# First matmuls on zeros counted at half clock in the plan, identity made on the chip, constants issued first, and the small matmuls on them later

## The chip, the cores and the metric

The kernel runs on one core of a Trainium2 chip. The time is the device time of one execution in microseconds (us). Eight runs of the kernel before gave a median of 177.66 us, the lowest 175.87 and the highest 178.57: six of them lie between 177.46 and 178.57, two at 175.87 and 176.14. One further execution was profiled; it took 177.76 us, of which the recorded span is 176.0 us.

A core has five engines that run side by side and wait for each other by semaphores: PE (TensorE; its weight loads are the row PEld), DVE (VectorE), ACT (ScalarE), POOL (GpSimd) and SP (SyncE, which here only issues transfers). Each engine takes its instructions in the order in which the program gives them, so an instruction that waits also holds up all that stands behind it.

## The reference

A retention layer is followed by a channel mix. Shapes: q, k, v are 4 batches x 8 heads x 768 steps x 64; the mix has a model width of 512 and an inner width of 1024.

```python
for t in range(S):
    state = gamma[None, :, None, None] * state + np.einsum('bhd,bhe->bhde', k[:, :, t], v[:, :, t])
    y[:, :, t] = scale * np.einsum('bhd,bhde->bhe', q[:, :, t], state)
...
x_prev = np.concatenate([np.zeros((B, 1, D), dtype=np.float32), x[:, :-1, :]], axis=1)
xk = mu_k * x + (1.0 - mu_k) * x_prev
xr = mu_r * x + (1.0 - mu_r) * x_prev
k = np.maximum(xk @ w_k, 0.0)
v = k * k @ w_v
r = 1.0 / (1.0 + np.exp(-(xr @ w_r)))
return (r * v).astype(np.float32)
```

## The kernel before

**Tiling.** Each batch is cut into six chunks of 128 steps, and the recurrence is done for two chunks at once, so there are 12 windows, here called w0 to w11. For a window, 512 KB each of k, q and v are loaded (L402). k and q are cast to half precision (L425 on DVE or L426 on ACT, `qks`), transposed on PE against an identity (L433), and copied out of PSUM (L443, `qkT`); v is multiplied by its decay (L456, on POOL or DVE). PE then forms the state (L475, L486; scaled by DVE at L499), the attention of each pair of steps (L519; masked by DVE at L536 with `causal2`), and the output (L561 from the state, L579 from the masked attention). DVE multiplies the output by `Gy` into `xT` (L599). One L579 is a Y below, with the window's number: Y0, Y1, Y2.

For the channel mix DVE forms the difference of neighbouring steps (`dx`, L623) and with `mu` the two mixed inputs `xk` and `xr` (L631). PE multiplies `xk` by `wk` (L662, "Z"), ACT takes the relu (L676, `krel`) and the square (L683, tile `k`); PE multiplies `xr` by `wr` (L695, "R"), ACT takes the sigmoid (L708, `rsb`); PE multiplies the squares by `wv` (L702, "V"), DVE multiplies both (L713, `osb`) and SP stores the result (L717).

**Weights.** `wk` comes in two halves, `wr` whole, `wv` in two halves: five transfers of 1024 KB (L376) into float32 tiles `w`, of which there are two (`w32=2`), so the third transfer needs the first tile cast, the fourth the second, and so on. A cast to half precision (L378 on DVE, L379 on ACT, L380 on POOL) fills a fifth of the weights that stay. The first V (L702) needs both halves of `wv`.

**Constants.** c32 (16 KB: the decays and a small identity `eye8`), c16 (96 KB: the 128x128 identity and the causal mask), c2 (9 KB) and two rows of mu (2 KB each) are issued by ACT's queue (L327). Two float32 matmuls on c2 (L358) and two copies (L361) make `Gy`; one transpose on `eye8` (L364) and a copy (L366) make `mu`.

**The plan.** No order is written out by hand. Tasks with a due time (`key`), buffers and ways (an engine, a duration, an added cost) are put to `Plan.order()`, which plays the program through with durations from the source and fixes, for each engine, the order of its instructions. `BUFS` says how many buffers of each kind there are, `COST` shifts the choice between engines, `FIRST` gives the due times of the first transfers, `LAT` the time that one engine's result takes to another, `STORE` by how much a store is put off, and `BLOCKS` how many chunks one channel-mix step takes in a batch. What is planned decides the order only; on the chip semaphores decide the time.

**Matmuls on zeros.** Where PE would stand idle in the first 60 us of the plan's time, `order()` puts in matmuls on a tile of zeros (`warm`, L280, a 128x256 one each), which nothing reads. They are there to hold the clock of PE. They are fixed in PE's order like the rest.

The lines that matter below:

```python
21  LA = (2, 0.3, 4)
66      FILL = 110
108             r = max(r, a.end + self.LAT[a.eng])
168                             f.start, f.end, f.eng = now, now + self.FILL, "PE"
269     ident = c16[:, 0:P]
435             e_T = add(key + 0.02 * i, pe(450, do_T), after=[e_c, k_c16] + hist[-1:], takes=[pT, xT],
```

## Time and profile before

| from the profile of the execution of 177.76 us | |
|---|---|
| span | 176.0 us, so 1.76 us lie outside it |
| PE busy | 167.1 us (95%), 2341 matmuls, of which 120 on zeros (17.5 us) |
| PE, 50 to 172 us | busy for 122.00 of 122.00 us, none of it on zeros |
| DVE busy | 131.5 us (75%) |
| ACT busy | 105.2 us (60%) |
| POOL busy | 37.6 us (21%) |
| bytes moved | 30.87 MB; 264 to 384 GB/s in the slices from 4.4 to 48.4 us, 129 GB/s on average from 50 to 172 us |
| first V (L702) | starts at 39.85 us |
| last matmul ends | 172.2 us |

The span is the time from the first recorded instruction to the last. A share of busy time is an average over all of it. The kernel has two parts that must be read apart: a head, in which PE fills its gaps with matmuls on zeros and waits, and a body, in which it does neither. In a row of a timeline the first number is the start in us, the second the duration of the group, then engine, line, operation, output, input and how many; in brackets stands how long the engine was idle before it and what ended that.

### The profile page before, as it was taken

The page shows a single profiled execution, that of the slowest core. Times are in us where ns is not written, and L with a number is a line of the kernel's source. Part 1 is how long each engine was busy: PE and PEld are TensorE (multiplying, and loading weights), DVE is VectorE, ACT ScalarE, POOL GpSimd, SP SyncE. Part 2 cuts the span into 40 slices and gives each one's busy share as a digit, 9 for nine tenths or more (in the row PEclk, how much of TensorE's full clock was granted, in tenths as well). Part 3 has the DMA queues.
Part 4 walks back from the last instruction along what each step waited for, and adds up shares of the span by engine and source line. Part 5 has one row for each costly group of instructions (what it writes and reads, how often), then busy time and mean ns, then how long its engine had stood idle before and what let it go on. Part 6 is the DMA issues. An engine that isn't in the chain of part 4 may idle for free.

```text
span 176.0 us, 5321 instructions
## 1 busy us (share of the span) xinstructions
PE 167.1 (95%) x2341; PEld 112.3 (64%) x2341; DVE 131.5 (75%) x230; ACT 105.2 (60%) x140; POOL 37.6 (21%) x32
## 2 busy tenths in 40 slices
PE   7959998989999999999999999999999999999991
PEld 5546877755855856856757747658567666775850
DVE  0024699988889999989888888798888499895311
ACT  2634254793692883983955936947829753646560
POOL 0035050492200344422003024240040040000000
PEclk9978999999999999999999999999999999999998
DMA  5999999999949656673393574846411011110202
GB/s 142 311 384 302 345 295 305 319 292 287 264 141 248 181 155 200 192 228 108 139 239 106 161 218 133 247 125 217 123 60 63 0 63 60 63 60 22 101 26 93
DMA packets 43866, 30.87 MB, mean 175 GB/s; under 512 B 1210, under 2 KB 38210, under 8 KB 43844
## 3 DMA queue, kind: packets, MB, share of 16 engines
q1 hardware_dynamic: 43536, 30.41, 58.7%
q8 instruction: 18, 0.29, 0.7%
q10 hardware_dynamic: 308, 0.13, 0.3%
q14 instruction: 4, 0.03, 0.1%
HBM read 24.25 MB, written 6.29 MB: 174 GB/s over the span
## 4 chain that ended last, share of the span: by engine, by line
PE 89%; POOL 4%; DVE 4%; issue 2%; DVEq 0%
PE pm L662 24%; PE pm L702 24%; PE pm L695 12%; PE pm L280 7%; PE px L433 6%; PE px L579 4%; PE px L486 4%; PE px L519 4%; PE px L561 3%; POOL wv L380 3%; DVE v L456 2%; POOL v L456 1%; PE pm L358 1%; DVE dx L623 1%; PE px L475 1%
## 5 line engine op out<-in xcount | busy, mean ns | idle before, releaser
L662 PE MATMUL pm<-xk,wk 128*128 128x256 f16 (+1 forms) x480 | 47.7, 251 | 0.0
L702 PE MATMUL pm<-wv,k 128*128 128x512 f16 x192 | 45.4, 379 | 0.6 <-POOL wv L380 0.6
L662 PEld LDWEIGHTS <-wk 128*128 128x128 f16 x480 | 38.2, 98 | 6.4
L443 ACT COPY qkT<-px 128x1024 f16<-128x1024 f16 x24 | 24.1, 1010 | 30.0 <-PE px L433 30.0
L676 ACT ACTIVATE krel<-pm 128x512 f32<-128x512 f32 x48 | 28.3, 596 | 19.0 <-PE pm L662 18.6
L456 POOL TENSOR_TENSOR v<-t,c_sb 128x512 f16<-128x512 f32 x20 | 20.5, 1046 | 77.5 <-issue 55.6
L536 DVE TENSOR_TENSOR a2t<-px,c_sb 128x512 f16<-128x512 f32 x48 | 30.7, 683 | 1.3 <-PE px L519 1.0
L702 PEld LDWEIGHTS <-k 128*128 128x128 f16 x192 | 17.8, 98 | 20.2 <-issue 0.7
L713 DVE SCALAR_TENSOR_TENSOR osb<-pm,rsb 128x512 f32<-128x512 f32 x24 | 16.6, 691 | 16.1 <-PE pm L702 8.5
L631 DVE SCALAR_TENSOR_TENSOR xr<-dx,mu,xT 128x256 f16<-128x256 f32 x48 | 22.6, 520 | 3.4 <-PE pm L695 3.3
L695 PE MATMUL pm<-wr,xr 128*128 128x512 f16 x96 | 24.8, 380 | 0.0
L426 ACT CAST qks<-t 128x1024 f16<-128x1024 f32 x19 | 19.7, 1041 | 6.0 <-DMA t<-in_k_dram 4.6
L683 ACT ACTIVATE k<-krel 128x1024 f16<-128x1024 f32 x21 | 22.2, 1059 | 0.5
L631 DVE SCALAR_TENSOR_TENSOR xk<-dx,mu,xT 128x256 f16<-128x256 f32 x48 | 21.4, 496 | 0.4
L280 PE MATMUL pm<-warm 128*128 128x256 f16 x120 | 17.5, 298 | 1.1 <-DVE xT L588 1.1
L708 ACT ACTIVATE rsb<-pm 128x512 f32<-128x512 f32 x24 | 14.2, 594 | 5.7 <-PE pm L695 5.5
L599 DVE TENSOR_TENSOR xT<-px,Gy 128x512 f32<-128x512 f32 x24 | 15.4, 683 | 1.9 <-PE px L579 1.6
L433 PEld LDWEIGHTS <-qks 128*128 128x128 f16 x192 | 13.2, 102 | 4.0
L623 DVE TENSOR_TENSOR dx<-xT 128x1024 f32<-128x1024 f32 x12 | 15.3, 1272 | 0.1
L433 PE MATMUL px<-c_sb,qks 128*128 128x128 f16 x192 | 15.3, 227 | 0.0
L280 PEld LDWEIGHTS <-warm 128*128 128x128 f16 x120 | 12.0, 106 | 3.9 <-DVE xT L588 1.1
L499 DVE TENSOR_TENSOR s<-px,c_sb 128x512 f16<-128x512 f32 (+1 forms) x12 | 7.2, 602 | 7.8 <-PE px L486 7.6
(30 smaller groups left out, 102.9 us busy)
## 6 DMA issues: line engine op xcount, KB each, us to landing
t<-in_k_dram SPq DMA_DIRECT2D x12, 512.0 KB, 5.3
t<-in_q_dram SPq DMA_DIRECT2D x12, 512.0 KB, 4.7
t<-in_v_dram SPq DMA_DIRECT2D x12, 512.0 KB, 4.6
out_dram<-osb SPq DMA_DIRECT2D x24, 256.0 KB, 2.5
w<-in_moe_w_k_dram SPq DMA_DIRECT2D x2, 1024.0 KB, 8.8
w<-in_moe_w_v_dram SPq DMA_DIRECT2D x2, 1024.0 KB, 8.7
w<-in_moe_w_r_dram SPq DMA_DIRECT2D x1, 1024.0 KB, 9.7
c_sb<-c ACTq DMA_DIRECT2D x1, 96.0 KB, 5.0
```

The source lines that it names most:

```text
L280: nc.tensor.matmul(b.tile[:, 0:256], lhsT=warm[:, 0:P], rhs=warm, start=True, stop=True)
L426: act(1010, lambda a=cast_args: nc.scalar.copy(**a()), cost=COST["qk"])],
L433: nc.tensor.transpose(o[:, j, m], x16.tile[:, j, m], ident)
L443: act(1010, lambda o=xT_out, pT=pT: nc.scalar.copy(out=o(), in_=pT.tile.bitcast(F16))),
L456: return lambda: engine.tensor_tensor(out=v16.tile[:, hs], in0=t32.tile[:, hs], in1=Gv[:, hs].unsqueeze(3).broadcast_to([P, 4, 2, D]), op= ...
L536: dve(690, lambda i=a_in, o=a_out: nc.vector.tensor_tensor(out=o(), in0=i(), in1=causal2, op=ALU.mult)),
L631: (200 + TM) / 0.96, lambda w=w, o=o, co=co: nc.vector.scalar_tensor_tensor(out=cut(o)[:, co], in0=cut(dx)[:, co], scalar=mu[:, w * NCO + ...
L662: nc.tensor.matmul(o[:, n], lhsT=wk16[:, co, fo * P : fo * P + P], rhs=cut(xk)[:, co, t0 : t0 + TM], start=(co == 0), stop=(co == NCO - 1))
L676: act(600, lambda pZ=pZ, o=r_out: nc.scalar.activation(out=o(), in_=pZ.tile, func=AF.Relu, scale=KSC)),
L683: act(1060, lambda krel=krel, k2=k2: nc.scalar.activation(out=k2.tile, in_=krel.tile, func=AF.Square)),
L695: nc.tensor.matmul(pR.tile, lhsT=cut(xr)[:, co, t0 + ts.start : t0 + ts.stop], rhs=wr16[:, co, :], start=(co == 0), stop=(co == NCO - 1))
L702: nc.tensor.matmul(pV.tile, lhsT=o[:, n, ts], rhs=wv16[:, fo, :], start=(fo == 0), stop=(fo == NFO - 1))
```

## The change

Durations, lines of code and tasks are changed together:

- A matmul on zeros that the plan puts in before 1500 + 3600 ns of its time counts as 220 ns there, later ones as 110 ns.
- The identity is made on the chip by POOL, by a memset and an `affine_select`, and no longer loaded; c16 holds the mask alone (64 KB). The transposes no longer wait for c16; the masking does.
- c32, c2, c16 and mu are issued in this order at the head of ACT's queue; in the plan their results count as 4500 ns late instead of 2000.
- The matmuls that make `Gy` and `mu` get later due times, and in w0 they come after the first attention matmuls (L519).
- `FIRST`, `BUFS`, `COST`, `STORE` and `BLOCKS` have other values. Among these: 3 tiles for loads of q, k, v (`t32`) instead of 5, 2 of `krel` instead of 4, 4 of `k2` instead of 6, 5 of `rsb` instead of 7, 3 of `osb` instead of 2, 3 of `qks` instead of 2. In batch 0 the channel mix of the first four chunks is done chunk by chunk, with Z as 128x128 matmuls.

The planned order changes with these. In PE's order 122 matmuls on zeros stand instead of 120, and the first V comes after the same other work as before, but with 64 Z of 128x128 in place of 32 of 128x256. The weights are cast by ACT (both halves of `wk`, `wr`, one half of `wv`) and POOL (the other half of `wv`); before, POOL cast all five. ACT casts 22 of the tiles of q and k instead of 19 and takes 41 relus instead of 48, DVE 7 instead of none; DVE copies 4 of the 24 `qkT`. SP's transfers stand in this order: k0 q0 v0 wk k1 q1 v1 wk k2 q2 wr v2 wv wv k3; before it was k0 q0 v0 wk wk k1 q1 v1 wr k2 q2 v2 wv wv k3 (the number is the window's).

```diff
@@ -19,14 +19,14 @@
 
 
 LA = (2, 0.3, 4)
-BLOCKS = {0: ((2,), (2,), (2,)), 3: ((1, 1), (1, 1), (1, 1))}
+BLOCKS = {0: ((1, 1), (1, 1), (2,)), 3: ((1, 1), (1, 1), (1, 1))}
 BLOCKS_ELSE = ((2,), (2,), (2,))
-STORE = 4
-FIRST = "k0 mu q0 c2 c16 v2 c32 v0 v1 q1 q2 wk1 wk0 k1 wr k2 wv1 wv0".split()
+STORE = 3
+FIRST = "c32 c2 c16 v1 q0 q2 q1 mu k0 v0 wk1 k1 wk0 k2 wr v2 wv1 wv0".split()
 BY_ACT = ("c2", "c16", "c32", "mu")
-BUFS = dict(t32=5, qks=2, v16=1, qkT=4, a2t=5, s16=2, xT=2, dx=3, xk=2, xr=1, krel=4, k2=6,
-            rsb=7, osb=2, w32=2)
-COST = dict(qk=-500, qkT=1200, relu=1200, mask=2000, dx=2000, v=200, w=-200, wd=500, sq=-500)
+BUFS = dict(t32=3, qks=3, v16=1, qkT=4, a2t=5, s16=4, xT=3, dx=2, xk=3, xr=2, krel=2, k2=4,
+            rsb=5, osb=3, w32=2)
+COST = dict(qk=0, qkT=300, relu=200, mask=800, dx=500, v=300, w=0, wd=800, sq=-200)
 
 
 class Buf:
@@ -48,7 +48,7 @@
         self.key, self.ways, self.mode, self.follows = key, ways, mode, follows
         self.after = [a for a in after if a is not None]
         self.takes, self.uses = list(takes), list(uses)
-        self.start = self.end = self.eng = self.emit = None
+        self.start = self.end = self.eng = self.emit = self.lat = None
 
 
 class Way:
@@ -63,7 +63,7 @@
     LAT = {"PE": 240, "ACT": 80, "DVE": 80, "POOL": 120, "DMA": 2000, "SP": 0}
     SWITCH = 100
     REACH = 1.2
-    FILL = 110
+    FILL, COLD = 110, 3600
 
     def __init__(self, filler, fill, fill_tag):
         self.tasks, self.bufs, self.makers = [], {}, {}
@@ -105,7 +105,7 @@
             for a in t.after:
                 if a.end is None:
                     return None
-                r = max(r, a.end + self.LAT[a.eng])
+                r = max(r, a.end + (a.lat or self.LAT[a.eng]))
             if any(not b.taken for b in t.uses):
                 return None
             for n, b in enumerate(t.takes):
@@ -165,7 +165,8 @@
                             f = Task(0, [], (), [b], (), "full", None)
                             r = ready(f)
                             if r is not None and r <= now:
-                                f.start, f.end, f.eng = now, now + self.FILL, "PE"
+                                slow = 2 if now < self.fill[0] + self.COLD else 1
+                                f.start, f.end, f.eng = now, now + self.FILL * slow, "PE"
                                 f.emit = lambda b=b: self.filler(b)
                                 b.users = 1
                                 finish(f, e)
@@ -252,7 +253,7 @@
         axis=1).astype(np.float32)
     causal_np = np.concatenate(
         [tq[None, :] >= (2 * (np.arange(P) % 64) + i)[:, None] for i in range(2)], axis=1)
-    c16_np = np.concatenate([np.eye(P), causal_np], axis=1).astype(np.float16)
+    c16_np = causal_np.astype(np.float16)
 
     const_pool = ctx.enter_context(tc.tile_pool(name="consts", bufs=1))
     c32d = nc.inline_tensor(c32_np, name="c32")
@@ -266,8 +267,8 @@
     c2 = const_pool.tile([2, c2_np.shape[1]], F32, name="c2_sb")
     Gy = const_pool.tile([P, 2, NJ, C], F32, name="Gy")
     eye8 = c32[0:8, o + 2 * NJ : o + 2 * NJ + 8]
-    ident = c16[:, 0:P]
-    causal2 = c16[:, P : P + 2 * C].unsqueeze(1).broadcast_to([P, 2, 2 * C])
+    ident = const_pool.tile([P, P], F16, name="ident")
+    causal2 = c16.unsqueeze(1).broadcast_to([P, 2, 2 * C])
     murow = const_pool.tile([8, P], F32, name="murow")
     mu = const_pool.tile([P, 8], F32, name="mu")
     wk16 = const_pool.tile([P, NCO, dff], F16, name="wk16")
@@ -329,7 +330,7 @@
     class Order:
 
 
-        eng = "SP"
+        eng, lat = "SP", None
 
         def __init__(self, t):
             self.t = t
@@ -342,6 +343,9 @@
         return FIRST.index(name) - 99.0 if name in FIRST else key
 
     nc.vector.memset(warm, 0.0)
+    nc.gpsimd.memset(ident, 0.0)
+    nc.gpsimd.affine_select(out=ident, in_=ident, pattern=[[1, P]], compare_op=ALU.not_equal,
+                            fill=1.0, base=0, channel_multiplier=-1)
     add(-97.0, act(0, lambda: nc.scalar.preload_act_table(AF.Sigmoid)))
     wkd = moe_w_k.rearrange("(co ci) f -> ci co f", ci=P)
     wvd = moe_w_v.rearrange("(fo fi) e -> fi fo e", fi=P)
@@ -352,18 +356,22 @@
     d0 = add(first("mu"), dma(50, murow[0:4], moe_mu_k.rearrange("(co ci) -> co ci", ci=P)))
     d1 = add(first("mu"), dma(50, murow[4:8], moe_mu_r.rearrange("(co ci) -> co ci", ci=P)))
     k_c2 = add(first("c2"), dma(50, c2, c2d.ap()))
-    k_gy = []
+    for t in (k_c32, k_c16, d0, d1, k_c2):
+        t.lat = 4500
+    k_gy, late = [], []
     for par in range(2):
         pG = Buf("pm")
-        e = add(-2.1, pe(900, lambda par=par, pG=pG: nc.tensor.matmul(
+        e = add(-1.78, pe(900, lambda par=par, pG=pG: nc.tensor.matmul(
             pG.tile, lhsT=c2[:, 0:P], rhs=c2[:, P + par * 512 : P + par * 512 + 512],
             start=True, stop=True)), after=[k_c2], takes=[pG], mode="full")
-        k_gy.append(add(-2.1, act(600, lambda par=par, pG=pG: nc.scalar.copy(
+        late.append(e)
+        k_gy.append(add(-1.78, act(600, lambda par=par, pG=pG: nc.scalar.copy(
             out=Gy[:, par].rearrange("p j t -> p (j t)"), in_=pG.tile)), after=[e], uses=[pG]))
     pmu = Buf("pm")
-    e = add(-2.0, pe(100, lambda: nc.tensor.transpose(pmu.tile[:, 0:8], murow, eye8)),
+    e = add(-1.75, pe(100, lambda: nc.tensor.transpose(pmu.tile[:, 0:8], murow, eye8)),
             after=[d0, d1, k_c32], takes=[pmu], mode="full")
-    k_mu = add(-2.0, act(170, lambda: nc.scalar.copy(out=mu, in_=pmu.tile[:, 0:8])),
+    late.append(e)
+    k_mu = add(-1.75, act(170, lambda: nc.scalar.copy(out=mu, in_=pmu.tile[:, 0:8])),
                after=[e], uses=[pmu])
 
     def weight(dkey, key, w16, wd):
@@ -432,7 +440,7 @@
                     for m in range(2):
                         nc.tensor.transpose(o[:, j, m], x16.tile[:, j, m], ident)
 
-            e_T = add(key + 0.02 * i, pe(450, do_T), after=[e_c, k_c16] + hist[-1:], takes=[pT, xT],
+            e_T = add(key + 0.02 * i, pe(450, do_T), after=[e_c] + hist[-1:], takes=[pT, xT],
                       uses=[x16], mode="full")
 
             def xT_out(xT=xT):
@@ -537,7 +545,7 @@
                         out=o(), in0=i(), in1=causal2, op=ALU.mult)),
                     act(590, lambda i=a_in, o=a_out: nc.scalar.copy(out=o(), in_=i()),
                         last=False, cost=COST["mask"])],
-                    after=[e_A] + ([Order(e_0)] if hp else []), takes=[] if hp else [a2t],
+                    after=[e_A, k_c16] + ([Order(e_0)] if hp else []), takes=[] if hp else [a2t],
                     uses=[pA[hp]] + ([a2t] if hp else []))
                 e_0 = e
                 e_m.append(add(key + 0.2 + 0.02 * st, pool(1000, lambda o=a_out: nc.gpsimd.tensor_tensor(
@@ -546,6 +554,9 @@
 
         e_A = attend(0, hist[-1:])
 
+        if g == 0:
+            for t in late:
+                t.after.append(Order(e_A))
         pY = [Buf("px"), Buf("px")]
 
         def y(cp):
```

## The prediction

> **What bounds the kernel now.** I read the windows of engine busy time first, then the chain of waits, then the timeline of the head and the groups with their releasers. The windows part the kernel in two (start:end, length, busy time of PE, PEld, DVE, ACT, POOL, PE's clock, DMA share, GB/s):
>
> ```profile
> 10.00:15.00 5.00, 4.12 (x43) 3.29 (x43) 1.29 (x2) 2.09 (x3) 3.02 (x2) 0.66 1.07 361
> ...
> 35.00:40.00 5.00, 4.24 (x83) 2.73 (x81) 4.44 (x7) 4.71 (x6) 4.80 (x3) 1.00 1.15 293
> ...
> 50.00:172.00 122.00, 122.00 (x1730) 79.86 (x1723) 99.57 (x176) 78.13 (x107) 22.10 (x19) 1.00 0.43 129
> ```
>
> From 50 to 172 us PE is never idle, and asking the same stretch for L280 alone gives 0.00 us. So the body is bound by PE, at full clock, and its length is its work. What a change can win or lose lies in the head, or in a stall that it brings into the body. The chain of waits shows where the head ends (start, length, what):
>
> ```profile
> 8.51 2.37 issue
> ...
> 20.97 0.69 DVE xT L599
> 21.69 1.24 DVE dx L623
> 22.97 0.06 issue
> 23.03 0.88 DVE xk L631 x2
> 23.91 2.91 DVE v L456 x2
> ...
> 33.09 2.04 POOL v L456 x2
> 35.13 4.68 POOL wv L380 x2
> 39.85 1.89 PE pm L702 x8
> 41.74 0.45 PE px L433 x8
> ```
>
> From 39.85 us on the chain is PE without a gap. The first V waits there for POOL, which casts both halves of `wv` one after the other, and which began only at 35.08 because it was busy with v until then. PE itself was ready earlier: the last attention matmul before that V ends at about 38.3, then come 7 matmuls on zeros and a wait. So the end of the kernel is set by **when the first V may start**: what moves it by one us moves the end by one us, if the work before it is the same and the body stays full. In the new order the same work stands before the first V (the transposes, states and attention of w0 to w2, two R, one batch of Z).
>
> **When can the first V start?** Four things: both halves of `wv` landed; both cast; the squares ready; PE through its earlier work.
>
> *Landing.* The DMA engines are busy all the time until 48 us. From the waits on transfers: k0 lands at 5.04, q0 at 6.75, the halves of `wk` at 11.55 and 14.29, k1 at 16.13, wr at 23.95, k2 at 25.78. So 512 KB take 1.7 to 1.84 us and a half weight 2.74. The first half of `wv` is issued at 23.87 and lands 8.7 later, at 32.6; the second by my estimate at 32.6 + 2.74 = 35.3. The change puts the transfers in another order, but ahead of the last half of `wv` stand the same thirteen: nine loads and four transfers of 1024 KB. So it lands at 35.3 again, unless the queue runs dry. It has fewer tiles (3 instead of 5 for q, k, v), so I walked each SP wait: k1 needs k0's cast (5.8), v1 needs v0's two products (9.9), k2 needs k1's cast (14.4, while k1 to `wk` fill the queue until 19.7), v2 needs v1's products (19.1, queue full to 27), the first `wv` half needs the second `wk` cast (21.6), the last needs wr's cast. wr lands two loads later than before, 23.95 + 2 x 1.8 = 27.5; ACT casts it until 29.4 (1.93, from ACT's 1.04 for 1024 and 0.60 for 512 elements). v2 and the first `wv` half keep the queue busy until 32.6, so this wait has 3 us of cover, less what a transfer needs to begin.
>
> *Here a rule stands against the row.* The Trainium skill, DMA: Bandwidth & Descriptors, section on the anatomy of one DMA (fitted for POOL's path), prices a transfer at about 2.0 us fixed plus its bytes at 436 GB/s: 4.4 us for a half weight. Issued at 29.5 it would land at 33.9. The rows say 8.3 to 9.7 us from issue to landing with the queue full, and 2.74 after its predecessor. By the rule the time is 1.4 us shorter than by the row; I take the row, since the queue is full here.
>
> *Cast.* POOL took 1.89 us for the second half and 2.89 for the first, which ran beside DVE's `dx`[...] (`dx` took 1.88 instead of 1.22). Now POOL has one half only, ACT the other (lands 32.6, cast until about 34.7). Around 35 to 37 DVE is at masks (L536), which did not slow the cast of 1.89, and one `xk`. So 2.0 us, at most 2.9. **First V: 35.3 + 2.0 + 0.1 = 37.4.**
>
> *PE's way there*, with durations of the rows. DVE casts k0 from 5.04 (0.68), PE transposes (0.5). The identity must stand by 5.8: a 128x128 memset and select on POOL, nearest rows 0.10 (tiny memset) and 1.05 (128x512 product), so 0.2 to 2.1 us from 0.4 on; hidden. q0's cast ends at 7.85, its transposes, after 15 zeros, at 8.6, its copy at 9.7; v0's products on DVE by 9.9. State and attention then end at 11.8. Before, the 16 transposes stood behind L364, which waited for c32: that is the 2.37 us of issue above. c32 (16 KB) was issued at 5.04 and used at 10.82, so took 5.8 us. Issued at 0.73 it is there by 6.5 at the same price, 2 us before its first use. L358 and L364 now come next, 1.92 + 0.24 us, at full price on PE, to 13.9; DVE's state (0.69) and two masks (1.29) lie beside them and end at 13.7, so about 0.2 us is uncovered. Then the second attention to 14.7, its masks to 16.2, Y0 at 16.2 (before: 19.61). In the same way POOL's v1 products end at 19.1, the second window's masks at 24.5, Y1 is at 24.9 (before: 32.33), first Z at 26.3 (28.26), wr's cast at 29.4, first R at 30.2 (33.78), last attention of w2 at 34.5 (38.3). DVE's copies of `qkT` have no row; between its 0.68 for a 128x1024 cast and 1.3 for two 128x512 reads of PSUM I took 1.0. ACT's queue behind wr's cast: two relus 30.7, a copy 31.7, a square 32.8, the `wv` half 34.7, sigmoid, relu, sigmoid 36.5, square 37.5. This is in time for the second V at 39.1, with 1.6 us to spare. So PE is ready 2.9 us before `wv`: the earlier start of the attention buys nothing by itself beyond 1.6 us (39.85 - 38.3), the split of the `wv` cast nothing beyond that without the other. Together they are worth 39.85 - 37.4 = 2.45 us.
>
> *The count of cold matmuls.* The first 8 zeros took 1.68 us (0.21 each), the next 28 3.86 (0.14), later ones 0.11. 36 of them thus cost 1.7 us more than at full clock. The Trainium skill, TensorE: Matmul & The Clock Gate, on what is actually happening, puts the ramp at under 1% of a kernel (up to 1.8 us here) and advises not to fit a count of cold matmuls. Either way all of it lies before 6.6 us, while transfers are awaited: zero in my sum. The plan merely lays 25 instead of 36 zeros ahead of the first real matmul.
>
> *The rest.* 64 Z of 128x128 cost 0.89 per 16, 32 of 256 0.87 to 0.98 per 8: zero. The clock of 0.66 above follows PE's idle stretch and goes with it, hidden too.
>
> **The body.** Same PE work, so its length stays if no new wait appears. DVE gains 7 relus (0.67 each by the plan's figure for it, near the 0.68 of L536) and 4 copies (about 1.0), and loses 3 casts (0.68): 131.5 + 6.7 = 138 us. ACT loses 7 x 0.60 + 4 x 1.01, gains 3 x 1.04 + 4 x 1.93: 105 + 2.6 = 108. Both stay below PE. With 3 tiles, k's load waits for v's products two windows back. In the new order k6 is issued at about 57.9 and lands 4.7 later at 62.6 (nearest rows: 4.6 to 5.3), while ACT has come to its cast at 61. Behind the cast waits the copy of k5's transposes, which PE makes at 63.7 only: 1 us of cover remains. q6 has 5 us. I put 0 in the sum. Sum: 177.76 - 2.45 = 175.3 us; the profiled execution lies 0.1 above the median, which I leave.
>
> **Rivals.**
> 1. *The cast or the landing is late.* POOL's cast beside DVE costs 2.9 and `wv` slips by half a us because its last half is issued late: V at 38.8, 176.7 us. For it: the row of 2.89, and wr's cast in the middle of ACT's queue. Against: DVE mostly reads PSUM then. Chance 0.17.
> 2. *`wv` comes sooner.* Before, wr landed 1.4 us later than the sum of its predecessors (14.29 + 3 x 1.84 + 2.74 = 22.55), perhaps since later loads ran alongside; now fewer are issued ahead. Then V is at 36.0, 173.9 us; the floor is PE at 34.7, 172.6 us. Against: bytes moved in the head are at 290 to 360 GB/s regardless. Chance 0.13.
> 3. *Slower: the body starves on three load tiles.* The place is ACT's cast of k, in order before relus and `qkT` copies; PE waits for those. The price: 0.5 us in each of the nine windows w3 to w11 is 4.5, less 2.45: 179.7 us. It decides from 2.45 / 9 = 0.27 us per window. For it: k's 1.6 us of waiting above, and only 2 `krel` and 4 `k2`. Against: cover of 1 us. Chance 0.20.
> 4. *It doesn't do what it says*: clock or constants turn out as before, but V still waits for `wv` alone; that is inside the forecast.
>
> **Numbers.** Forecast 175.3, chance 0.50, its own range 174.5 to 176.3. A measurement of this kernel tells apart about 0.5%, that is 0.89 us: faster means below 176.8. The forecast, rival 2 and half of rival 1 are faster: 0.50 + 0.13 + 0.08 = 0.71. Of the rest, rival 1's other half and the mild part of rival 3 lie within: 0.11; slower 0.18. The range runs from 173.0, most of rival 2, to 178.4, the mild part of rival 3.
>
> **What would show it.** First V near 37.4 with POOL's `wv` cast as its releaser, begun on a landing; Y0 near 16; no long PE gap before 10; no zeros after the first V and PE busy without a gap to 169.7. It is wrong if ACT's casts in the body wait for loads and PE's idle then names ACT, if SP stands idle on a cast while the DMA share falls below 1 before 35 us, or if the first V waits for a square instead of `wv`.

## Result, and the profile after

| us | before | after |
|---|---|---|
| median | 177.56 (55 runs, 175.53 to 178.72) | 175.81 (20 runs, 174.98 to 178.62) |
| profiled execution | 177.76 | 175.88 |
| its span, and the time outside it | 176.0 and 1.76 | 173.7 and 2.18 |
| first V starts | 39.85 | 37.54 |
| last matmul ends | 172.2 | 169.98 |
| from the first V to there | 132.35 | 132.44 |

The time became 0.9922 of what it was, 95% interval 0.9893 to 0.9950. The ratio leaves out executions that lie over 1.5% above the lowest of their kernel, the medians do not.

The times of the kernel before form groups: 13 at 175.5 to 176.1, 32 at 177.4 to 177.8 and 10 at 178.5 to 178.7. For 57 executions of it that were run beside the experiments the mean granted clock of PE is on record, and it parts the same groups: 15 at 175.6 to 176.0 had 0.996 to 0.999, 35 at 177.4 to 177.9 had 0.986 to 0.990, 7 at 178.5 to 178.7 had 0.981. In the profile (0.987) the clock is low from 10 to 15 us, and both profiles are of the middle group, so whether and how the clock makes these 2.0 us is not shown. Of the kernel after, the five executions at 0.999 or 1.000 took 174.98 to 175.17, the other fifteen (0.977 to 0.990) 174.99 to 178.62 with a median of 176.1. At like clocks the change is thus worth about 0.6 us where the clock stays full and about 1.5 where it does not. The account below compares profiles with a mean clock of 0.987 and 0.990.

The page's rows of busy time of the kernel after (busy us, share of the span, instructions), and its group of V's (busy and mean ns of one, then PE's idle time before it and who ended it):

```profile
PE 166.9 (96%) x2407; PEld 113.0 (65%) x2407; DVE 134.7 (78%) x238; ACT 108.1 (62%) x136; POOL 28.9 (17%) x30
...
L713 PE MATMUL pm<-wv,k 128*128 128x512 f16 x192 | 45.3, 379 | 1.5 <-POOL wv L388 1.5
```

All idle time before 192 V matmuls is one wait of 1.5 us for POOL's cast of `wv`. The lines have moved: V is L713 now, a weight is loaded at L384 and cast at L387 (ACT) or L388 (POOL), a zero is L281. The chain of waits (start, length, what) shows the same place in time:

```profile
35.46 2.04 POOL wv L388
37.49 0.04 issue
37.54 3.61 PE pm L713 x16
41.15 0.45 PE px L441 x8
```

Before, the cast took 4.68 us from 35.13 on, both halves, behind v. Now POOL has one half, begins when it lands, and takes 2.04. Between these two profiles that is the gain: 39.85 - 37.54 = 2.31 us.

The windows of busy time (start:end, length, PE, PEld, DVE, ACT, POOL, clock of PE, DMA share, GB/s) answer for head and body:

```profile
15.00:20.00 5.00, 5.00 (x67) 3.83 (x66) 2.15 (x4) 1.96 (x2) 1.43 (x2) 0.71 1.09 342
...
35.00:40.00 5.00, 3.45 (x46) 1.87 (x41) 3.23 (x6) 3.83 (x5) 2.03 (x1) 1.00 1.07 277
50.00:100.00 50.00, 50.00 (x775) 33.08 (x774) 44.76 (x78) 35.85 (x47) 10.08 (x9) 1.00 0.63 182
100.00:169.60 69.60, 69.60 (x947) 45.75 (x945) 55.52 (x98) 40.35 (x55) 11.97 (x10) 1.00 0.35 103
```

From 50 to 169.6 us PE is busy without a gap at full clock, as before: the smaller buffers brought no stall. PE's head can be followed in the timeline (start, length of the group, operation; in brackets the idle time before it):

```profile
5.76 0.62 PE L441 MATMUL px<-ident,qks 128*128 128x128 f16 x8 [0.28 <-DVE qks L433]
...
15.29 2.56 PE L281 MATMUL pm<-warm 128*128 128x256 f16 x11
...
17.78 0.66 PE L590 MATMUL px<-a2t,v 64*64 64x128 f16 x32
...
26.70 0.64 PE L590 MATMUL px<-a2t,v 64*64 64x128 f16 x32
```

The first transposes wait for DVE's cast of k0 and not for the identity, which POOL made from 0.73 to 1.30 us. Ahead of Y0 (17.78) stand 11 zeros of 0.23 us each, double the 0.11 of the plan: they fall into a stretch of low clock (0.71 over these 5 us), and they are fixed in PE's order. Y0 is 1.6 us later than forecast, and Y1 (26.70) 1.8.

### The profile page after: what moved, and what is told of

It is laid out like the page before. It is cut to its first block, busy times and chain, and to the rows that moved or that the text cites. A ratio compares the mean times of both kernels' runs of the same rounds, so it can differ in the third digit from the quotient of the medians.

```text
span 173.7 us, 5463 instructions
## 1 busy us (share of the span) xinstructions
PE 166.9 (96%) x2407; PEld 113.0 (65%) x2407; DVE 134.7 (78%) x238; ACT 108.1 (62%) x136; POOL 28.9 (17%) x30
## 4 chain that ended last, share of the span: by engine, by line
PE 82%; issue 9%; DMA 3%; POOL 2%; ACT 1%; DVE 0%; SPq 0%; DVEq 0%; POOLq 0%
PE pm L713 24%; PE pm L673 23%; PE pm L706 11%; PE px L441 6%; PE px L590 4%; PE px L494 4%; PE px L527 3%; DMA t<-in_q_dram 3%; PE pm L281 3%; PE px L572 2%; POOL v L464 1%; POOL wv L388 1%; PE pm L364 1%; ACT qks L434 1%; PE px L483 1%
## 5 line engine op out<-in xcount | busy, mean ns | idle before, releaser
L673 PE MATMUL pm<-xk,wk 128*128 128x128 f16 (+1 forms) x544 | 48.2, 241 | 0.0
L713 PE MATMUL pm<-wv,k 128*128 128x512 f16 x192 | 45.3, 379 | 1.5 <-POOL wv L388 1.5
L673 PEld LDWEIGHTS <-wk 128*128 128x128 f16 x544 | 39.5, 98 | 5.2
L687 ACT ACTIVATE krel<-pm 128x512 f32<-128x512 f32 x41 | 24.4, 597 | 20.1 <-PE pm L673 19.6
L713 PEld LDWEIGHTS <-k 128*128 128x128 f16 x192 | 18.0, 98 | 21.6 <-issue 1.5
L451 ACT COPY qkT<-px 128x1024 f16<-128x1024 f16 x20 | 20.2, 1009 | 18.6 <-PE px L441 18.6
L434 ACT CAST qks<-t 128x1024 f16<-128x1024 f32 x22 | 23.0, 1045 | 7.4 <-DMA t<-in_q_dram 4.3
L281 PE MATMUL pm<-warm 128*128 128x256 f16 x122 | 18.6, 304 | 1.1 <-DVE xT L599 1.1
L441 PE MATMUL px<-ident,qks 128*128 128x128 f16 x192 | 15.1, 223 | 0.5 <-DVE qks L433 0.3
L281 PEld LDWEIGHTS <-warm 128*128 128x128 f16 x122 | 12.3, 108 | 4.2 <-DVE xT L599 1.1
L441 PEld LDWEIGHTS <-qks 128*128 128x128 f16 x192 | 12.2, 100 | 3.7 <-DVE qks L433 0.6
L706 PEld LDWEIGHTS <-xr 128*128 128x128 f16 x96 | 8.5, 98 | 7.0
```

What stands on the lines that cost most here:

```text
L281: nc.tensor.matmul(b.tile[:, 0:256], lhsT=warm[:, 0:P], rhs=warm, start=True, stop=True)
L434: act(1010, lambda a=cast_args: nc.scalar.copy(**a()), cost=COST["qk"])],
L441: nc.tensor.transpose(o[:, j, m], x16.tile[:, j, m], ident)
L451: act(1010, lambda o=xT_out, pT=pT: nc.scalar.copy(out=o(), in_=pT.tile.bitcast(F16))),
L673: nc.tensor.matmul(o[:, n], lhsT=wk16[:, co, fo * P : fo * P + P], rhs=cut(xk)[:, co, t0 : t0 + TM], start=(co == 0), stop=(co == NCO - 1))
L687: act(600, lambda pZ=pZ, o=r_out: nc.scalar.activation(out=o(), in_=pZ.tile, func=AF.Relu, scale=KSC)),
```

## Experiments

There are twelve. All but `before_2`, which is a single execution, are compared with the kernel before on the same chip; "profile" is the time of the profiled execution, and behind a ratio stands its 95% interval. The kernel after was run once more unchanged.

> The changed kernel once more, for a second profile and times on the same chip as the next three. Theory (the end is set by the start of the first V, which is set by the landing and cast of the last half of wv): first V again between 37.2 and 37.8 us, last matmul 132.4 us later, whatever the clock did in the head. Rival (PE's way through the head sets it, so its clock does): the start of the first V differs from 37.5 by as much as Y1 differs from 26.7 us.

Median 176.02 (6 runs), ratio 0.989 (0.9782 to 0.9998). The granted clock was 1.00 throughout, the 11 zeros took 1.36 us instead of 2.56, and Y0 came at 16.50. Then PE waited 1.68 us for POOL's products for v, so Y1 came at 27.29, 0.6 later than in the first profile; the first V came at 37.17, 0.4 earlier. Differences of this size on PE do not carry over to V here. `before_2`, a second profile of the kernel before, was to catch its lower group:

> The kernel before once more, to see what its several times (groups near 175.6, 177.6 and 178.6 us) are made of. Theory: the first V follows the end of POOL's second wv cast, and POOL starts its casts when it has done v, which waits for Y1; so if this execution is one of about 175.6, Y1 lies about 2 us sooner than 32.3 us, and first V about 2 us sooner than 39.85; if it is one of 177.6, both stand as before. Rival (the body differs): first V at 39.85 whatever the time.

It took 177.8 with V at 39.91 and a mean clock of 0.988, the middle group again, so its question stays open.

### Does the end hang on the landing and cast of `wv`?

`wv_small` transfers a quarter of the last half of `wv` (256 KB) and casts that quarter four times over; its output is another.

```diff
+        def got():
+            return wide()[:, 0:1] if small else wide()
...
+        def cast_in():
+            return wide()[:, 0:1].broadcast_to(list(w16.shape)) if small else wide()
...
+        d = add(dkey, Way("DMA", 2600, lambda: nc.sync.dma_start(out=got(), in_=wd[:, 0:1] if small else wd)), takes=[w32])
...
+            pool(1900, lambda: nc.gpsimd.tensor_copy(out=w16, in_=cast_in()), cost=COST["w"])],
```

> The changed kernel, but the last half of wv transfers a quarter of its rows (256 KB in place of 1024 KB) and casts them four times over, so those weights are not the reference's; instructions and their order stay. 0.75 of a transfer of 2.74 us falls away: the landing moves from 35.4 to about 33.4 us, the cast ends at about 35.5, and PE, ready at 36.0 us, becomes the bound. Theory: first V at about 36.0, so 1.5 us sooner, and the end 1.5 us sooner than in the changed kernel (about 174.3 in the profiled execution against 175.9). Rival (wv is not the bound): first V and end stay.

Profile 173.60, median 173.93, ratio 0.9824 (0.9739 to 0.9909). The timeline's cast:

```profile
32.50 1.89 POOL L394 CAST wv<-w 128x2048 f16<-128x2048 f32 x1 [12.11 <-DMA w<-in_moe_w_v_dram]
```

It begins 3.0 us sooner than in the kernel after (35.46). V gains only 2.1, to 35.43, since PE comes to it no sooner and does not wait for it at all. The end of the last matmul follows, from 169.98 to 167.81. So the landing does set the end, with 2.1 us to win below it; I had expected 1.5, since I put PE's own readiness at 36.0.

`wv_twice` makes POOL cast its half twice.

```diff
-            pool(1900, lambda: nc.gpsimd.tensor_copy(out=w16, in_=wide()), cost=COST["w"])],
+            pool(1900, lambda: [nc.gpsimd.tensor_copy(out=w16, in_=wide()) for _ in range(2)], cost=COST["w"])],
```

> The changed kernel, but POOL casts its half of wv twice in a row, to the same place. Nothing else moves. Theory: the first V starts 1.9 to 2.0 us later (39.5) and the end is later by the same, 177.8 in the profiled execution, which is back at the time before the change. Rival (slack in the body takes it up): less than 1 us.

Profile 180.61, median 180.65, ratio 1.0205 (1.0119 to 1.0291): 4.7 us more than the kernel after, where I expected 1.9. Timeline and windows:

```profile
36.55 3.97 POOL L388 CAST wv<-w 128x2048 f16<-128x2048 f32 x2 [16.18 <-DMA w<-in_moe_w_v_dram]
...
40.57 5.42 PE L713 MATMUL pm<-wv,k 128*128 128x512 f16 x16 [5.17 <-POOL wv L388]
```

```profile
36.00:45.00 9.00, 4.43 (x13) 1.65 (x13) 1.55 (x4) 2.31 (x3) 3.91 (x2) 0.62 0.83 225
```

The second cast is worth 1.9. The transfer landed 1.1 later in this execution. And behind 5.17 us of waiting PE's clock was at 0.50 from 38 to 44 us (0.62 over the window), so 16 V took 5.42 instead of 3.61, another 1.8. The sum is 4.8: a longer wait costs PE its clock on top of the wait.

`v_turned` lets the first two V begin with the half of `wv` that lands first and is cast by ACT.

```diff
             def do_V(pV=pV, ts=ts):
-                for fo in range(NFO):
+                fos = [4, 5, 6, 7, 0, 1, 2, 3] if b == 0 and c0 < 2 else range(NFO)
+                for i, fo in enumerate(fos):
...
-                                     start=(fo == 0), stop=(fo == NFO - 1))
+                                     start=(i == 0), stop=(i == NFO - 1))
```

> The changed kernel, but the first two V take the rows of wv in the order 4 to 7, 0 to 3 in place of 0 to 7. The half of wv that lands last holds rows 0 to 3, so the first four matmuls of the first V no longer wait for it. Theory: they run from 36.0 to 36.9 while the cast goes on, the fifth waits to 37.5; the end comes 0.9 us sooner than in the changed kernel (about 175.0 in the profiled execution). Rival (PE is not ready at 36.0, or the second V is then held up by its square): 0.3 us or less.

Profile 174.14, median 175.05, ratio 0.9886 (0.9813 to 0.9960). Timeline:

```profile
35.11 1.02 PE L714 MATMUL pm<-wv,k 128*128 128x512 f16 x4
36.77 2.75 PE L714 MATMUL pm<-wv,k 128*128 128x512 f16 x12 [0.63 <-POOL wv L388]
```

Four matmuls (1.02 us) go ahead of the end of the last cast, and 0.63 us of waiting is left. In this execution the half also landed 0.6 sooner (the cast began at 34.82), so of the 1.7 us by which the profile is shorter about 1.0 is the order's. The medians differ by 0.8, and the intervals of the two ratios overlap. The three agree: in the kernel after, the last cast of `wv` before the first V sets the end.

### Which part of the change brings it?

`retune` has the new `BLOCKS`, `STORE`, `BUFS` and `COST`, but the old `FIRST`, constants, identity, due times and count of zeros. `named` is the reverse: the parts that the change is named for, with the new `FIRST` and the old values of the rest.

```diff
 retune, against the kernel before
-BLOCKS = {0: ((2,), (2,), (2,)), 3: ((1, 1), (1, 1), (1, 1))}
+BLOCKS = {0: ((1, 1), (1, 1), (2,)), 3: ((1, 1), (1, 1), (1, 1))}
-STORE = 4
+STORE = 3
-BUFS = dict(t32=5, qks=2, ...
+BUFS = dict(t32=3, qks=3, ...
-COST = dict(qk=-500, qkT=1200, ...
+COST = dict(qk=0, qkT=300, ...
```

> Only the numbers of buffers, costs, blocks and the store's delay of the change; identity and constants as before, c32 issued late, nothing counted cold. PE again stands for about 2.4 us before the first transposes, but ACT casts both halves of wv and nothing holds it at the landing. Theory: first V between 37.3 and 38.4, 175.9 to 176.8 us in the profiled execution. Rival (the stall on c32 is what the change gains): no better than before, 177.5.

> Only the parts that the change names: cold matmuls counted at half clock, identity on the chip, constants first and counted late, small matmuls later, with the new due times of the first transfers; all buffer numbers, costs, blocks and the store's delay as before. POOL still casts all weights, but takes the second half of wv when it lands, since w2's v has gone to DVE. In the planned order 15 zeros in place of 2 and one more set of transposes and one Y (1.0 us) stand right before the first V: PE is ready at about 36.0 + 1.0 + 1.4 = 38.4, with 1.0 us less to do behind it. Theory (the two sets of edits are two ways to the same bound, wv's landing plus one cast): as the changed kernel, 175.9 us in the profiled execution, between 175.0 and 176.6. Rival (the gain needs the new buffers and costs): 177.5.

`retune`: profile 176.68, median 176.67 (all ten within 0.55 us), ratio 0.9978 (0.9939 to 1.0018). `named`: profile 178.83, median 178.39, ratio 1.0050 (0.9996 to 1.0103), outside what I expected. First `retune`, then `named`, in the timeline:

```profile
35.48 1.90 ACT L379 CAST wv<-w 128x2048 f16<-128x2048 f32 x1 [0.37 <-DMA w<-in_moe_w_v_dram]
37.57 3.63 PE L702 MATMUL pm<-wv,k 128*128 128x512 f16 x16
```

```profile
38.21 1.70 PE L281 MATMUL pm<-warm 128*128 128x256 f16 x14
...
40.84 0.63 PE L590 MATMUL px<-a2t,v 64*64 64x128 f16 x30 [0.31 <-DVE a2t L544]
41.41 1.90 PE L713 MATMUL pm<-wv,k 128*128 128x512 f16 x8
```

In `named`, with the old values, POOL still casts both halves, each as it lands (31.73 to 34.06 and 36.62 to 38.51), and even after that V waits: 14 zeros, transposes and w2's attention stand ahead of it in PE's order, and the masks come late. In `retune` ACT casts both halves, the second until 37.38, and PE comes to V at 37.57 without a wait, as in the kernel after.

Neither part alone is told apart from the kernel before: both intervals take in 1. How the gain divides between them stays open. That `retune` moves V because POOL is rid of the `wv` casts is read from its trace, not isolated: it has other values of everything else too. And all its ten executions had a mean clock of at least 0.996; those of the kernel before at that clock took 175.6 to 176.0, which is less. The whole change is 0.8 us better than `retune` in the profile. There the last matmul ends at 170.75, 0.75 us more behind the same V, though PE has no gap in either; two zeros behind V are 0.2 of it, the rest is open.

### Constants, zeros and their price, each taken out of the whole

`const_old` keeps the order of the kernel after. The identity comes by a transfer, and c32 is issued behind ACT's first cast. That cast is q0's here, so c32 is issued at 7.00 and not at 5.04 as in the kernel before, and v0's products start at 11.68 instead of 10.82: it makes c32 later than the change found it.

```diff
+    identd = nc.inline_tensor(np.eye(P).astype(np.float16), name="ident_in")
...
-    nc.gpsimd.memset(ident, 0.0)
-    nc.gpsimd.affine_select(out=ident, ...)
...
-    k_c32 = add(first("c32"), dma(100, c32, c32d.ap()))
-    k_c16 = add(first("c16"), dma(200, c16, c16d.ap()))
+    k_c32 = add(first("c32"), Way("DMA", 100, lambda: None))
+    late_c32 = [lambda: nc.scalar.dma_start(out=c32, in_=c32d.ap())]
+    k_c16 = add(first("c16"), Way("DMA", 200, lambda: [nc.scalar.dma_start(out=ident, in_=identd.ap()),
+        nc.scalar.dma_start(out=c16, in_=c16d.ap())]))
...
-                act(1010, lambda a=cast_args: nc.scalar.copy(**a()), cost=COST["qk"])],
+                act(1010, lambda a=cast_args: (nc.scalar.copy(**a()), late_c32 and late_c32.pop()()), cost=COST["qk"])],
```

> The changed kernel, its order kept, but the identity is loaded by a transfer of its own on ACT's queue instead of made by POOL, and c32 is issued behind ACT's first cast, as before the change. By the rows of the kernel before the identity lands at about 7 us (first transposes at 7 in place of 5.76) and c32 about 5.8 us after 8.3, that is at 14: v0's products on DVE at 14.0 in place of 8.83, so the first state and attention end some 4 us later. Theory: slack and the waits for k1, v1 and wr take up most; first V between 37.4 and 39, time between 175.6 and 177.2. Rival 1 (constants do not matter at all): as the changed kernel to 0.2 us. Rival 2 (all of it goes through): 4 us slower.

Profile 177.99, median 179.28, ratio 1.0097 (1.0053 to 1.0142): 2.1 us slower than the kernel after in the profile, 3.5 in the median, where I expected at most 177.2. The identity was in time: the first transposes came at 5.84 instead of 5.76, so making it on the chip gains nothing that shows here. c32 was not, and the timeline shows the way from there to V:

```profile
11.68 1.29 DVE L464 TENSOR_TENSOR v<-t,c_sb 128x512 f16<-128x512 f32 x2 [4.51 <-DMA c_sb<-c]
...
29.43 1.01 ACT L451 COPY qkT<-px 128x1024 f16<-128x1024 f16 x1 [3.65 <-PE px L441]
30.34 1.90 ACT L387 CAST wr<-w 128x2048 f16<-128x2048 f32 x1
...
38.02 1.89 POOL L388 CAST wv<-w 128x2048 f16<-128x2048 f32 x1 [13.36 <-DMA w<-in_moe_w_v_dram]
```

DVE waits 4.5 us for c32, PE's attention slips by that and by a stretch behind it at a clock of 0.50 (16 to 22 us), to Y1 at 30.75, so ACT's copy of `qkT` waits 3.65 us for PE. Behind it in ACT's queue stands the cast of `wr`, and on that cast waits the issue of the last `wv` half. The waits of SP's queue (who, for whom, total, times, longest) and the window of 30 to 36 us say the same; first the two rows of the kernel after:

```profile
SPq L384 <- ACT wr L387: 1.9, 1, 1.9
```

```profile
30.00:36.00 6.00, 5.99 (x117) 4.36 (x115) 5.47 (x10) 5.86 (x8) 0.54 (x1) 1.00 0.94 280
```

Then those of `const_old`:

```profile
SPq L384 <- ACT wr L387: 4.9, 1, 4.9
```

```profile
30.00:36.00 6.00, 6.00 (x108) 5.27 (x106) 5.60 (x12) 4.65 (x6) 0.00 (x0) 1.00 0.49 184
```

SP holds the issue 3 us longer and the queue runs dry: half the DMA share, 184 GB/s instead of 280. From the end of `wr`'s cast to the start of POOL's cast of `wv` it is 6.13 us in the kernel after (29.33 to 35.46), 5.97 in its second profile, and 5.78 here (32.24 to 38.02). So V slips by 2.4 us, and the profile by 2.1.

`nocold` counts every zero at 110 ns (`FILL, COLD = 110, 0`), so 42 zeros instead of 25 stand ahead of the first real matmul.

> The changed kernel with cold matmuls on zeros counted at 110 ns again. In the planned order this does one thing: 42 zeros stand ahead of the first transposes in place of 25. In the kernel before the 36th ended at 6.59 us and later ones take 0.11, so the 42nd ends at about 7.2 and the first transposes start there, not at 5.76: 1.4 us late. Theory: PE's way to the first V has about 1.5 us of slack besides the fixed zeros, so first V stays within 0.4 us of 37.5 and the time at 175.5 to 176.3. Rival (the head's start goes through to the end): 1.4 us slower than the changed kernel.

Profile 176.59, median 176.15, ratio 0.9930 (0.9892 to 0.9968). The chain is the same, milder: Y0 19.77, Y1 29.08, ACT's copy waits 2.10 us for PE, `wr`'s cast ends at 30.58, POOL's cast begins 5.84 later:

```profile
36.42 1.89 POOL L388 CAST wv<-w 128x2048 f16<-128x2048 f32 x1 [13.42 <-DMA w<-in_moe_w_v_dram]
```

The 42 zeros took 7.65 us, 0.18 each, so the first transposes began at 8.54 and not at the 7.2 expected. V is 0.8 later (I expected 0.4 at most), the profile 0.7 longer. The medians differ by 0.34 (176.15 and 175.81) and the ratios' intervals overlap, so the count alone is not settled by the times; the route is shown by the trace.

`no_zeros` emits none of the matmuls on zeros.

```diff
     def filler(b):
-        nc.tensor.matmul(b.tile[:, 0:256], lhsT=warm[:, 0:P], rhs=warm, start=True, stop=True)
+        pass
```

> The changed kernel without its 122 matmuls on zeros. PE's way to the first V has 1.5 us of slack, and from 28 to 36 us PE has real work without zeros. Theory: the head runs partly at half clock, but first V moves by 0.7 us at most and the body stays at full clock: at most 0.7 us slower than the changed kernel. Rival (the clock in the head matters): first V at 38.5 or later, or the first V at half clock, as they ran in the kernel that casts wv twice (5.42 us for 16 in place of 3.61): 1.8 us slower or more.

Median 175.52, ratio 0.9939 (0.9885 to 0.9993): not apart from the kernel after. Six runs lie at 175.06 to 175.55 and four at 176.74 to 177.16. The profile (176.74) is of the second kind:

```profile
37.09 5.03 PE L713 MATMUL pm<-wv,k 128*128 128x512 f16 x16 [2.71 <-POOL wv L388]
```

V starts 0.45 sooner than with zeros, but behind 2.71 us of idling the clock is at 0.50 from 37 to 40 us, and its 16 matmuls take 5.03 us instead of 3.61. The price of 1.42 is near the distance between the two kinds, 1.7 us between their middles; that the first kind keeps the clock was not profiled, and the mean clocks do not part them (0.979 to 1.000 and 0.976 to 0.989). In the head the price of having no zeros shows: the first transposes take 1.03 us instead of 0.62, the two float32 products for `Gy` 3.77 instead of 1.98. But no zeros stand in the way either, and nearly all of Y0 comes at 17.76, as with them (17.78).

### Two more

`before_v2` changes one thing in the kernel before: w2's product for v moves from POOL to DVE, so that POOL is free for `wv`.

```diff
-                pool(1000, v_decay(nc.gpsimd)),
+                pool(1000, v_decay(nc.vector if (b, w) == (0, 2) else nc.gpsimd)),
```

> The kernel before, but the two products of w2's v, which POOL makes at 33.09 to 35.13 us ahead of its two wv casts, go to DVE at the same place of the order. POOL is then free when wv lands: casts 32.6 to 34.6 and 35.3 to 37.3. PE is ready at 38.3. Theory: first V at 38.3 to 39.2, so 0.6 to 1.5 us sooner than 39.85, and the end by the same; not more, since PE's own way then binds. Rival ([...]v's products read two tiles of SBUF on DVE beside POOL's casts, as when one took 2.38 us in place of 0.69): the states and masks behind them come late and first V is at 39.85 or later.

The ten runs spread from 175.63 to 181.32 (median 179.42, ratio 0.9949, 0.9886 to 1.0011), and the profile is of the longest, so the number decides nothing. It shows where the wait went in that execution, which is the rival's way:

```profile
36.71 2.91 DVE L623 TENSOR_TENSOR dx<-xT 128x1024 f32<-128x1024 f32 x1
...
40.01 0.63 PE L561 MATMUL px<-qkT,s 64*64 64x128 f16 x16 [2.29 <-DVE s L499]
```

POOL casts `wv` earlier, but beside it (36.30 to 38.55) DVE's `dx` takes 2.91 instead of 1.22, the state behind it is late, and PE waits for that. The first V came at 42.14, behind the 2.29 us of waiting, and its 8 matmuls took 3.16 us instead of 1.89, at a clock of 0.50. Whether the shorter executions go another way was not profiled.

`v_halves` goes on from `v_turned`: the first two V give their matmuls on the early half of `wv` first, both, then those on the late half (the lines left out let `do_V` take a range of rows and set its start and stop by it).

```diff
...
     plan.order()
+    (e_0, V_0), (e_1, V_1) = firsts
+    lo, hi = range(4), range(4, 8)
+    e_0.emit = lambda: V_0(hi)
+    e_1.emit = lambda: (V_1(hi), V_0(lo), V_1(lo))
```

> The changed kernel, but the first two V are done by halves: rows 4 to 7 of wv for both chunks, in two banks, then rows 0 to 3 for both. The half that lands last is needed 1.8 us after the first V starts in place of at once. Theory: with PE ready at about 35.1 (as when the rows were turned), 8 matmuls run to 36.9 while POOL casts, and the wait is 0.2 us or none; the end comes about 0.7 us sooner than with turned rows, 1.6 sooner than the changed kernel: 173.4 to 174.6 us. Rival (the second chunk's square, ready at about 36.8, holds its first half): no better than turned rows, 175.05.

Profile 174.59, median 174.63 (4 runs), ratio 0.9879 (0.9789 to 0.9968).

```profile
35.56 1.99 PE L714 MATMUL pm<-wv,k 128*128 128x512 f16 x8
35.80 1.89 POOL L388 CAST wv<-w 128x2048 f16<-128x2048 f32 x1 [15.19 <-DMA w<-in_moe_w_v_dram]
...
37.74 1.89 PE L714 MATMUL pm<-wv,k 128*128 128x512 f16 x8 [0.20 <-POOL wv L388]
```

The transfer landed 0.3 later in this execution, and still only 0.20 us of the wait remains. Its median is the lowest of the kernels that compute the reference, 1.2 us below the kernel after; but its interval overlaps that kernel's, and `v_turned` is 0.4 behind it, which four runs each do not tell apart.

## Why the prediction was right, and where it was not

**The sum.** Forecast 175.3, measured 175.81, profile 175.88. In the sum's own terms: PE ends at 169.98, not 169.75 (+0.23), and the time outside the span is 2.18, not 1.76 (+0.42). I took that as unchanged. It is 2.18 in `retune` and 2.23 in `named`, 1.89 in `const_old` and 1.80 in `before_2`; what sets it stays open. The mechanism, that the first V waits for the landing and one cast of `wv` and sets the end, is what the runs show. That the number came so close is in part luck, as the next steps tell.

**First V 37.4** (measured 37.54). Landing 35.3 against 35.46 and 35.23 in the two profiles, cast 2.0 against 2.03 and 1.89. Rival 1's cast of 2.9 beside DVE did not come, and neither did rival 2's earlier landing. The 2.74 us from one half's landing to the other's is not a constant: it was 2.77 in `retune` (32.71 to 35.48), but 4.27 in `before_v2` (32.03 to 36.30) and 4.89 in `named` (31.73 to 36.62).

**Row against rule.** The row was right. By the rule of the Trainium skill (DMA: Bandwidth & Descriptors, the anatomy of one DMA, fitted for POOL's path) the estimate was 4.4 us from issue to landing, which would have put V at 36.0. SP's issue of that half ends at 29.72 and the cast begins at 35.46, 5.7 us. `wv_small`, 256 KB, took 2.6 us less than 1024 KB from the end of `wr`'s cast (3.37 against 5.97 in the second profile). As an estimate from these two: 768 KB (0.786 MB) in 2.6 us is 302 GB/s, beside the loads of the next window, and what is left is 2.5 us. The fixed part is near the rule's 2.0; the rate isn't 436.

**"This wait has 3 us of cover"** is the step that failed, at no cost to the sum. `wr`'s cast ended at 29.33 as predicted (29.4), but the transfer issued behind it needs 5.8 to 6.1 us from there to land (in six executions of this order; 6.5 in `v_halves`, 7.4 in `wv_twice`), so the cover was gone: 29.4 + 5.9 is 35.3, the same time that the flow of bytes gives. In `retune` `wr` is cast from 24.02 to 25.92, the last half is issued by 26.41, and it lands at 35.48 all the same. Two limits stand at one time, and I saw only one; that they agree is luck. The sign that I had named against the forecast was there: SP waited 1.9 us for `wr`'s cast, and the DMA share was below 1 before 35 us (0.94 over 30 to 36 us, 0.79 with 182 GB/s over the first two of them). Hence also **"the earlier start of the attention buys nothing by itself beyond 1.6 us"** misleads: a late head delays ACT's copy, `wr`'s cast, the issue and V, which costs 2.1 us in `const_old`. Rival 1 named this route ("wr's cast in the middle of ACT's queue"); without the delay that rival 1 adds, it is the forecast's own.

**PE's way** was forecast too quick: Y0 17.78 and not 16.2, Y1 26.70 and not 24.9, first R 31.39 and not 30.2. I had struck out the zeros between real matmuls; 11 of them took 2.56 us. And the low clock, which I took to go away with PE's idle stretch, was there without one: 0.61 from 14 to 16 us and 0.53 from 16 to 18, with PE busy all the time from 10 on. Nor was it hidden in the kernel before, if the groups of its times are what their clocks suggest. POOL's cast still came last, by 1.5 us instead of the 2.9 predicted. "PE ready at 34.5" became about 36.0 with its zeros; in `no_zeros` PE is done with the attention at 34.4 (37.09 - 2.71), so the zeros are the term that was left out.

**The cold count at zero** is not borne out. The reason, all of it before 6.6 us while transfers are awaited, does not hold: 17 more zeros there moved Y1 by 2.4 us and V by 0.8, so it is worth 0.7 us between the profiles. The medians differ by 0.34, which the noise leaves open.

**The body at zero**: right. ACT waits for loads in it, which is what the forecast named as a sign against itself:

```profile
ACT qks L434 <- DMA t<-in_k_dram: 2.0, 3, 1.0
...
ACT qks L434 <- DMA t<-in_q_dram: 0.7, 1, 0.7
```

From 40 us on that is 2.7 us in four waits, 1.0 at most, and none reached PE, which has no gap there. So rival 3 did not occur, though its first step did. DVE's 134.7 and ACT's 108.1 us answer to the 138 and 108 predicted; a DVE copy of `qkT` took 0.69, not 1.0.

## What to carry to other kernels

Where one transfer waits for a buffer to be cast, follow it as a chain of its own: the queue position of the cast, the issue, the full time from issue to landing, and only then ask for its cover. Where several limits stand at one time, taking one away shows little, and each still costs nearly in full when it gets later (in `const_old` an issue 2.9 us later moved V by 2.4). An accumulation over a weight that comes in parts can begin with the part that is there: in `v_halves` that hid all but 0.20 us of the last wait.

## What the runs showed that I had not expected

- PE's clock came down behind short waits: to 0.50 behind 1.57 us in `named`, 2.29 in `before_v2` and 2.71 in `no_zeros`, where the next 16 V took 5.03 us instead of 3.61. It stayed at 1.00 behind 1.55 us in the kernel after and 1.68 in `after_2`. The Trainium skill, TensorE: Matmul & The Clock Gate, section on why this matters for your kernels, advises against idle gaps of over about 3 us; here shorter ones went ahead of a low clock. And in the kernel after and `nocold` it fell to 0.50 with PE busy all the time before. The length of the gap alone thus does not decide it; what else does is open.
- Taking out the matmuls on zeros, meant to hold the clock, changes nothing that the times tell apart (median 175.52 without, 175.81 with).
- `dx` on DVE took 1.22 us alone and up to 2.91 beside POOL. In eight slowed cases, beside casts as well as products for v, it ended 1.07 to 1.09 us after the POOL instruction that it met, however long that still had to run: it took nearly its whole time only after that was done, instead of sharing. In the kernel before, `dx` so waited for the product for v until 35.13, and the first `wv` cast in turn ran 1.0 us longer beside it.
